# Attention and gated feed-forward on one core: a new place in VectorE's order for three helpers of each unit's last block

## The chip, the cores and the metric

The kernel runs on one core of a Trainium2 chip. The metric is the device time of one execution in microseconds (us), lower is better. The engines are TensorE (PE in the profile, with PEld for its weight loads), VectorE (DVE), ScalarE (ACT), GpSimd (POOL) and SyncE (SP), which issues the transfers.

## The reference, cut to what matters

Attention over 8 batches, 8 heads, 576 positions and 64 values a head, in which a query sees only the 32 keys up to itself (heads 0 to 3) or every fourth of the 128 keys up to itself (heads 4 to 7). Its output, 4608 tokens of 512 values, goes through an RMS norm and a gated feed-forward layer with 1536 hidden values.

```python
scores = where(mask, q @ k.T / 8, -1e9)
x = softmax(scores) @ v                       # to 4608 x 512
xn = x / sqrt(mean(x * x) + 1e-6) * rms_g
g, val = xn @ w_gate, xn @ w_val
out = (g * sigmoid(g) * val) @ w_out
```

## The kernel before, in words

**Units and slots.** The tokens are cut into 16 units u of 288 (half a batch). A unit's feed-forward layer runs over 12 hidden blocks j of 128 values, and each j has three slots of TensorE's order: part 0 is `gate` (12 matmuls into the tile g), part 1 is `val` (12 matmuls into v), part 2 is `proj` of the hidden block before (12 matmuls into four accumulators). At the end of a slot `attend` may add matmuls of the attention of the next unit, so that attention of one unit lies beside the feed-forward layer of the one ahead of it. Each product of the feed-forward layer and, from unit 3 on, of the attention is made of a high and a low part of its operands, which other engines split.

**The order.** It is written out by hand. `later(dt, rank, fn)` (line 435) puts a helper into the list of the slot that is dt slots on; `flush` (line 438) issues that list at the slot's start, sorted by rank, so rank alone decides in which order VectorE and ScalarE get the helpers of one slot. Every engine works through its own list in that order and waits where an operand is not there. What follows a waiting instruction on its engine waits too.

**The hidden block's helpers.** After `gate` of j come, one slot on, the tanh (rank 0, ScalarE, line 816) and `silu` (rank 0.6, VectorE, line 821), both out of g in PSUM; after `val`, one slot on, come `prod` (rank 0, VectorE, line 834: the product of h, th times v) and `parts` (rank 0.5: ScalarE's copy to the high part hhi, line 845, and GpSimd's subtraction to hlo, line 846). The two PSUM banks of g and v alternate: `bank` (line 788) gives g of block j + 1 the bank that v of block j has. So TensorE's first matmul of the next `gate` waits until `prod` has read v.

**The attention's helpers.** A unit has 14 blocks (c, i): for c = 0 and 1 three blocks of 96 queries, for c = 2 and 3 four of 72, each for two heads. A block goes through scores (matmul into the tile s), the softmax's maximum, exponential and normalisation, a transposition of the probabilities, and the output matmul into o. `take` (line 429) sums the parts of o into xraw: from unit 3 on two VectorE instructions for each head (lines 447 and 449), four for a block, at the slot after the output; behind a part-2 slot they have ranks 0.1 and 0.3.

**The turned blocks.** For units 3 to 15 and the blocks (3, 1), (3, 2) and (3, 3) TensorE doesn't transpose; `turn` (line 505) does it with VectorE's transposes of 32 x 64 tiles into a PSUM tile z. In a unit with an even u the band of 72 keys takes 5 such turns a block, with an odd u, where the keys are 104, it takes 6. `turn` is called in the slot of the transposition and leaves three helpers: `squares_of` (VectorE's turns, line 520, one slot on with rank 9, so last in that slot), `hi` (ScalarE's copy of z to the high part of pt, line 525, two slots on, rank 0.2) and `lo` (VectorE's subtraction to the low part of pt, line 529, two slots on, rank 0.9). TensorE's output matmul (line 571) takes both parts. The unit's plan (lines 54 to 60 and 921 to 929) sets these slots, counted from part 0 of j = 0:

| block | turn called | `squares_of` | `hi`, `lo` | output | `take` |
|---|---|---|---|---|---|
| (3, 1) | 17 (part 2) | 18 | 19 | 21 (part 0) | 22 |
| (3, 2) | 19 (part 1) | 20 | 21 | 23 (part 2) | 24 |
| (3, 3) | 21 (part 0) | 22 | 23 | 25 (part 1) | 26 |

Slot 22 is part 1 and slot 23 part 2 of j = 7. The `prod` of j = 7 is in slot 23 with rank 0, `silu` of j = 7 in slot 22 with rank 0.6, and `silu` of j = 8 in slot 25. The turns of block (3, 3) thus stand on VectorE between `silu` and `prod` of j = 7.

The lines that the prediction's steps touch: 429 to 449 (`take`), 505 to 535 (`turn`), 571 (output), 775 and 778 (the matmuls of `gate`, `val`, `proj`), 816 to 846.

Of the kernel before, what the change touches and what calls it, by code (L numbers as in the profile page):

```python
# [62 lines left out]
def geometry(u, c):  # L63


    half = u % 2
    if c < NC // 2:
        if half:
            return [(QB * i, QB * i, 0, P) for i in range(U // QB)], QB, U + W
        return [(QB * i, max(QB * i - W, 0), 0 if i else W, P if i else QB)  # L70
                for i in range(U // QB)], QB, U
    nq = U // DIL
    keys = nq + (W if half else 0)
    return [(nq * r, keys * r, 0 if half else W, keys) for r in range(DIL)], nq, keys * DIL
# [3 lines left out]
def attn_moe(ctx: ExitStack, tc: tile.TileContext, qk_in, v_in, w_gate, w_val, w_out, rms_g, outT):  # L78
# [41 lines left out]
    def later(dt, rank, fn):  # L120
        put_off.setdefault(now[0] + dt, []).append((rank, fn))
# [383 lines left out]
    def turn(b, p):  # L505
        u, c, i = b
        _, nq, _ = geometry(u, c)
        n = geometry(u, c)[0][i][3]
        ng = math.ceil(nq / 32)

        def clear():
            squares_ps[u] = ps.tile([P, 512], F32, tag="s", name=f"z_{u}")[:, :2 * QB].rearrange("k (a q) -> k a q", a=2)
            A.activation(out=squares_ps[u], in_=inv[:, :, None].to_broadcast([P, 2, QB]), func=AF.Copy, scale=0.0)

        def squares_of():
            z = squares_ps[u]
            for g in range(ng):
                for k in (g, g + 1) if u % 2 else (g - 1, g):
                    if k >= 0:
                        V.transpose(out=z[32 * k:32 * (k + 1), :, 32 * g:32 * (g + 1)],  # L520
                                    in_=p[32 * g:32 * (g + 1), :, 32 * k:32 * (k + 1)])

        def hi():
            st[b] = pt = sb.tile([P, 2, 2, QB], F32R, tag="pt", name=f"pt_{u}_{c}_{i}", bufs=2)
            A.copy(out=pt[:n, 0, :, :nq], in_=squares_ps[u][:n, :, :nq])

        def lo():
            pt = st[b]
            V.tensor_tensor(out=pt[:n, 1, :, :nq], in0=squares_ps[u][:n, :, :nq], in1=pt[:n, 0, :, :nq], op=ALU.subtract)

        if i == 1:
            later(1, 7, clear)
        later(1, 9, squares_of)
        later(2, 0.2, hi)
        later(2, 0.9, lo)

    def products(q, t, o, t_ps, s_tag="s", o_tag="o", wait=0):

# [9 lines left out]
        if by_squares:  # L548
            turn(t, p)
# [501 lines left out]
```

## Time and profile before

| | |
|---|---|
| runs | 1111.31, 1114.48, 1116.33 us; median 1114.48 us |
| the profiled execution | 1117.7 us, span 1115.9 us, mean granted clock of TensorE 0.993 |
| busy, share of the span | PE 98%, PEld 96%, DVE 76%, POOL 60%, ACT 56% |
| transfers | 82.18 MB, mean 74 GB/s |

The profiled execution's own time is 1.8 us over its span, and 3.2 us over the median of the runs. Start times in the rows below count from the span's start. In a row of a timeline the columns are start (us), length (us), engine, line, operation, what it writes and reads, shapes and count; a bracket at the end gives the engine's idle time before the instruction and what ended it. Matmuls are pipelined: their lengths overlap, and the distance between their starts is what each costs.

### The profile page before, as it was taken

The numbers are of one execution on the slowest core, as the hardware profiler recorded it, in microseconds if no ns is written. First come the engines' busy times: TensorE is split into PE (matmuls) and PEld (weight loads), VectorE is DVE, ScalarE is ACT, GpSimd is POOL, SyncE is SP. The second block draws the span as 40 slices with busy tenths as digits, with TensorE's granted clock in tenths as the row PEclk, the third lists the DMA queues.
The fourth block names the chain that finished last, engine by engine and source line by source line (L and its number), as shares of the span: only waits on it lengthen the run. The fifth ranks groups of instructions, "written<-read, shape, count | busy, mean of one in ns | idle before, by whom it ended". The sixth has DMA issues, their size and how long they took to land.

```text
span 1115.9 us, 25579 instructions
## 1 busy us (share of the span) xinstructions
PE 1092.2 (98%) x8234; PEld 1067.0 (96%) x8234; DVE 848.9 (76%) x3348; ACT 625.1 (56%) x2241; POOL 672.0 (60%) x1126
## 2 busy tenths in 40 slices
PE   9999999999999999999999999999999999999998
PEld 7787999999999999999999999999999999999998
DVE  6889667878788787887778787787878878788411
ACT  6794676546475564646556464664647556464311
POOL 6333589657585575857657585775758657584311
PEclk9999999999999999999999999999999999999999
DMA  9674213212121121312212131130312112120000
GB/s 257 191 257 171 76 52 91 70 33 81 43 92 52 35 89 42 94 40 58 79 39 84 41 86 52 48 96 26 89 42 87 57 32 86 50 71 13 13 11 22
DMA packets 61544, 82.18 MB, mean 74 GB/s; under 512 B 7298, under 2 KB 41090, under 8 KB 61410
## 3 DMA queue, kind: packets, MB, share of 16 engines
q1 hardware_dynamic: 61410, 80.54, 24.0%
q8 instruction: 66, 1.08, 0.4%
q14 instruction: 68, 0.56, 0.2%
HBM read 71.08 MB, written 9.44 MB: 72 GB/s over the span
## 4 chain that ended last, share of the span: by engine, by line
PE 82%; DVE 13%; issue 2%; ACT 2%; POOL 1%; POOLq 0%; DVEq 0%; ACTq 0%
PE g L778 14%; PE acc L778 14%; PE v L778 14%; PE g L775 8%; PE acc L775 7%; PE v L775 7%; DVE z L520 5%; PE s L583 3%; PE o L571 2%; DVE xraw L447 2%; PE acc L772 2%; PE v L772 2%; PE g L772 2%; DVE xraw L449 2%; PE t L556 1%
## 5 line engine op out<-in xcount | busy, mean ns | idle before, releaser
L846 POOL TENSOR_TENSOR hlo<-th,hhi 128x288 fp32r<-128x288 f32 x179 | 145.1, 811 | 170.6 <-ACT hhi L845 153.3
L425 POOL TENSOR_SCALAR t<-t,sum 96x128 f32<-96x128 f32 (+3 forms) x416 | 150.8, 375 | 112.8 <-DVE sum L419 97.0
L409 ACT ACTIVATE t<-t,sum 96x128 f32<-96x128 f32 (+3 forms) x448 | 166.1, 374 | 92.1 <-DVE sum L394 86.8
L778 PE MATMUL acc<-hhi,lo 128*128 128x288 f32 x720 | 212.5, 295 | 0.0
L778 PE MATMUL g<-xhi,lo 128*128 128x288 f32 x612 | 181.8, 297 | 0.0
L778 PE MATMUL v<-xhi,lo 128*128 128x288 f32 x612 | 181.6, 297 | 0.0
L816 ACT ACTIVATE th<-g 128x288 f32<-128x288 f32 x180 | 74.1, 411 | 173.3 <-PE g L778 132.0
L821 DVE SCALAR_TENSOR_TENSOR th<-th,g 128x288 f32<-128x288 f32 x180 | 80.9, 449 | 96.0 <-ACT th L816 77.4
L447 DVE TENSOR_REDUCE xraw<-o 64x72 f32<-64x144 f32 (+1 forms) x364 | 116.9, 321 | 47.6 <-PE o L571 42.2
L778 PEld LDWEIGHTS acc<-hhi,lo 128*128 128x128 f32 x720 | 135.3, 188 | 0.0
L775 PE MATMUL g<-xhi,hi_g 128*128 128x288 f32 x357 | 108.7, 304 | 16.8 <-DVE th L834 16.8
L845 ACT CAST hhi<-th 128x288 fp32r<-128x288 f32 x180 | 77.7, 432 | 76.9 <-DVE th L834 76.8
L324 POOL TENSOR_TENSOR vhl<-vt,vhl 128x128 fp32r<-128x128 f32 x182 | 84.2, 463 | 59.1 <-ACT vhl L320 30.9
L778 PEld LDWEIGHTS v<-xhi,lo 128*128 128x128 f32 x612 | 116.0, 190 | 0.0
L778 PEld LDWEIGHTS g<-xhi,lo 128*128 128x128 f32 x612 | 115.9, 189 | 0.0
L449 DVE TENSOR_TENSOR xraw<-o,xraw 64x72 f32<-64x72 f32 (+1 forms) x364 | 101.2, 278 | 12.5
L775 PE MATMUL acc<-hhi,hi_o 128*128 128x288 f32 x360 | 107.8, 299 | 0.0
L778 PE MATMUL acc<-hlo,hi_o 128*128 128x288 f32 x360 | 106.5, 296 | 0.0
L834 DVE TENSOR_TENSOR th<-th,v 128x288 f32<-128x288 f32 x180 | 79.8, 443 | 32.3 <-PE v L778 31.7
L363 POOL TENSOR_TENSOR qs<-qk,qs 64x288 fp32r<-64x288 f32 x104 | 84.1, 809 | 19.7 <-ACT qs L358 12.4
L778 PE MATMUL g<-xlo,hi_g 128*128 128x288 f32 x322 | 95.9, 298 | 0.0
L354 POOL TENSOR_TENSOR ks<-qk,ks 128x288 fp32r<-128x288 f32 (+2 forms) x104 | 93.3, 902 | 2.1
(203 smaller groups left out, 3508.9 us busy)
## 6 DMA issues: line engine op xcount, KB each, us to landing
qk<-in_qk_dram SPq DMA_DIRECT2D x60, 288.0 KB, 2.8
vt<-in_v_dram SPq DMA_DIRECT2D x196, 64.0 KB, 1.9
qk<-in_qk_dram SPq DMA_DIRECT2D x30, 352.0 KB, 3.0
out_dram<-ot SPq DMA_DIRECT2D x64, 144.0 KB, 1.9
qk<-in_qk_dram SPq DMA_DIRECT2D x30, 304.0 KB, 2.7
raw<-in_w_gate_dram SPq DMA_DIRECT2D x12, 512.0 KB, 4.6
raw<-in_w_val_dram SPq DMA_DIRECT2D x12, 512.0 KB, 3.3
raw<-in_w_out_dram SPq DMA_DIRECT2D x12, 512.0 KB, 4.1
```

Source lines behind the costliest of these rows:

```text
L324: G.tensor_tensor(out=vp[:, :, 1], in0=vs.pop(b), in1=vp[:, :, 0], op=ALU.subtract)
L354: ek.tensor_tensor(out=ks[:, 1, :nkt], in0=kr, in1=ks[:, 0, :nkt], op=ALU.subtract)
L363: eq.tensor_tensor(out=qs[D:], in0=qr[D:], in1=qs[D:], op=ALU.subtract)
L409: A.activation(out=t[:nq, a, :n], in_=t[:nq, a, :n], func=AF.Exp, scale=-1.0, bias=sm[:nq, a, 0:1], accum_out=None if by_rows(u, c, i) els ...
L425: (V if u == 0 and (c, i) > (NC - 1, 1) else G).tensor_scalar(out=t[:nq, a, :n], in0=t[:nq, a, :n], scalar1=sm[:nq, a, 3:4], scalar2=1.0, ...
L447: V.tensor_reduce(out=ours, in_=o[:D, cols:cols + 2 * nq].rearrange("d (t q) -> d q t", t=2), axis=mybir.AxisListType.X, op=ALU.add)
L449: V.tensor_tensor(out=ours, in0=o[D:, cols:cols + nq], in1=ours, op=ALU.add)
L775: PE.matmul(out, wh[:, cc, :], xh, start=start, stop=False)
L778: PE.matmul(out, w[:, cc, :], v, start=False, stop=stop and k == 1)
L821: V.scalar_tensor_tensor(out=t, in0=t, scalar=1.0, in1=g, op0=ALU.add, op1=ALU.mult)
L834: V.tensor_tensor(out=t, in0=t, in1=v_ps[:, :U], op=ALU.mult)
L846: (V if (u, j) == (NU - 1, NJ - 1) else G).tensor_tensor(out=lo, in0=t, in1=hi, op=ALU.subtract)
```

## The change: what it does

For the last block of each unit, (3, 3), the three helpers of `turn` get other slots and ranks. For block (3, 1) and (3, 2) nothing changes.

```diff
-        later(1, 9, squares_of)
-        later(2, 0.2, hi)
-        later(2, 0.9, lo)
+        last = i == len(geometry(u, c)[0]) - 1
+        later(1 + last, 0.1 if last else 9, squares_of)
+        later(2, 0.55 if last else 0.2, hi)
+        later(2 + last, 0.58 if last else 0.9, lo)
```

In slots: `squares_of` of the last block goes from the end of slot 22 to slot 23 with rank 0.1, just behind `prod`; `hi` stays in slot 23 and goes behind ScalarE's hhi copy; `lo` goes to slot 24 with rank 0.58, behind both halves of `take` of block (3, 2).

## Rows read from the trace of the kernel before

**Rows 1.** The page: busy time by engine, and the chain that ended last

```profile
PE 1092.2 (98%) x8234; PEld 1067.0 (96%) x8234; DVE 848.9 (76%) x3348; ACT 625.1 (56%) x2241; POOL 672.0 (60%) x1126
...
PE 82%; DVE 13%; issue 2%; ACT 2%; POOL 1%; POOLq 0%; DVEq 0%; ACTq 0%
```

**Rows 2.** Waits of PE: line and waited for, us in total, times, longest

```profile
PE g L775 <- DVE th L834: 16.8, 13, 1.7
```

**Rows 3.** Timeline of PE, two units with six turns a block

```profile
361.23 0.35 PE L571 MATMUL o<-pt,vhl 104*128 104x144 f32 x2
361.42 0.34 PE L775 MATMUL v<-xhi,hi_g 128*128 128x288 f32 x1
...
361.86 0.29 PE L775 MATMUL v<-spare,hi_g 128*128 128x288 f32 x1
...
498.96 0.34 PE L571 MATMUL o<-pt,vhl 104*128 104x144 f32 x2
501.02 0.40 PE L775 MATMUL g<-xhi,hi_g 128*128 128x288 f32 x1 [1.71 <-DVE th L834]
...
501.52 0.30 PE L775 MATMUL g<-xhi,hi_g 128*128 128x288 f32 x1
...
504.31 0.35 PE L571 MATMUL o<-pt,vhl 104*128 104x144 f32 x2
```

**Rows 4.** Timeline of PE, a unit with five turns a block

```profile
432.83 0.34 PE L571 MATMUL o<-pt,vhl 72*128 72x144 f32 x2
433.97 0.40 PE L775 MATMUL g<-xhi,hi_g 128*128 128x288 f32 x1 [0.80 <-DVE th L834]
...
434.48 0.30 PE L775 MATMUL g<-xhi,hi_g 128*128 128x288 f32 x1
```

**Rows 5.** Timeline of DVE, the six-turn unit at 500 us

```profile
497.03 0.29 DVE L447 TENSOR_REDUCE xraw<-o 64x72 f32<-64x144 f32 x1
...
498.31 0.45 DVE L821 SCALAR_TENSOR_TENSOR th<-th,g 128x288 f32<-128x288 f32 x1
498.78 1.70 DVE L520 STREAM_TRANSPOSE z<-t 32x64 f32<-32x64 f32 x6
500.51 0.45 DVE L834 TENSOR_TENSOR th<-th,v 128x288 f32<-128x288 f32 x1
500.88 0.30 DVE L529 TENSOR_TENSOR pt<-z,pt 104x144 fp32r<-104x144 f32 x1
```

**Rows 6.** Timeline of DVE, the five-turn unit at 433 us

```profile
432.04 1.40 DVE L520 STREAM_TRANSPOSE z<-t 32x64 f32<-32x64 f32 x5
433.46 0.45 DVE L834 TENSOR_TENSOR th<-th,v 128x288 f32<-128x288 f32 x1
```

**Rows 7.** Timeline of ACT, the six-turn unit at 500 us

```profile
500.51 0.28 ACT L525 CAST pt<-z 104x144 fp32r<-104x144 f32 x1 [3.25 <-DVE z L520]
```

**Rows 8.** Timeline of PE, the six-turn unit at 366 us

```profile
366.70 0.51 PE L775 MATMUL g<-xhi,hi_g 128*128 128x288 f32 x1 [1.71 <-DVE th L834]
...
370.32 0.30 PE L775 MATMUL v<-spare,hi_v 128*128 128x288 f32 x1
```

**Rows 9.** Windows: stretch, length, busy PE, PEld, DVE, ACT, POOL, clock, DMA, GB/s

```profile
200.00:250.00 50.00, 48.29 (x366) 48.13 (x366) 38.67 (x160) 25.09 (x93) 27.91 (x50) 0.97 0.16 45
...
350.00:400.00 50.00, 48.29 (x365) 48.14 (x364) 39.20 (x159) 26.83 (x100) 31.05 (x53) 0.97 0.20 57
400.00:1000.00 600.00, 589.15 (x4616) 587.71 (x4615) 484.61 (x2009) 342.16 (x1267) 397.57 (x680) 1.00 0.21 62
1000.00:1050.00 50.00, 48.28 (x364) 48.14 (x363) 36.25 (x139) 18.86 (x69) 19.97 (x36) 0.97 0.03 9
```

**Rows 10.** Timeline of DVE, the six-turn unit, behind the wait

```profile
503.42 0.46 DVE L821 SCALAR_TENSOR_TENSOR th<-th,g 128x288 f32<-128x288 f32 x1 [1.06 <-ACT th L816]
...
510.51 0.43 DVE L834 TENSOR_TENSOR th<-th,v 128x288 f32<-128x288 f32 x1
```

**Rows 11.** Timeline of PE, the six-turn unit, the gate after the next

```profile
511.57 0.29 PE L775 MATMUL g<-xhi,hi_o 128*128 128x288 f32 x1
```

## The prediction

> **What bounds the kernel now.** I read the page first. TensorE is busy 98% of the span and holds 82% of the chain that ended last [rows 1]; an edit on VectorE can pay only where TensorE stands still. VectorE's 13% of that chain is the lead: there are places where the chain leaves TensorE. The list of TensorE's waits names the place: 13 times the first matmul of a gate waits for the product of h, 16.8 us in all [rows 2]. Units 3 to 15 are 13, seven with six turns a block and six with five. In a six-turn unit the wait is 1.71 us [rows 3, 8], in a five-turn unit 0.80 us [rows 4], and 7 x 1.71 + 6 x 0.80 = 16.8: one wait a unit, always in slot 24, whose gate needs the bank that the product of j = 7 must first read.
>
> VectorE's timeline shows why. Behind silu, at 498.31, come the six turns of the last block, 498.78 to 500.48, and only then the product, 500.51 to 500.96 [rows 5]. TensorE's gate starts 0.06 us after that, at 501.02 [rows 3]. The turns aren't needed until the output of slot 25, so they hold up the earlier deadline for the later one.
>
> **What a wait costs, by starts.** Unhindered, the group behind an output pair starts 361.42 - 361.23 = 0.19 us after it, and its first three matmuls take 0.44 us [rows 3]. In the six-turn unit the gate starts 2.06 us after the pair (498.96 to 501.02), 1.87 late, and its first three take 0.50 (to 501.52) [rows 3]: 1.93 us lost. In the five-turn unit it starts 1.14 after (432.83 to 433.97), 0.95 late, and 0.51 for the first three [rows 4]: 1.02 lost. Sum: 7 x 1.93 + 6 x 1.02 = 13.5 + 6.1 = **19.6 us**.
>
> **What the clock adds.** After the wait at 366 us the next five threes of matmuls take 370.32 - 366.70 = 3.62 us [rows 8], where an unslowed unit takes 0.50 + 4 x 0.40 = 2.10; 0.40 is the step of 12 matmuls from 361.42 on, three at a time, and of the span 501.52 to 504.31, seven threes in 2.79 [rows 3]. So 1.52 us more. The granted clock says what it is: 0.97 in just those three 50 us stretches that hold a six-turn wait followed by slow matmuls, and 1.00 over the 600 us from 400 on [rows 9], in which waits of both kinds lie. [...] 3 x 1.52 = **4.6 us**, which goes if the wait does.
>
> **What the change adds, part by part.**
> The product starts where the turns started: 498.78, ends 0.45 later at 499.23, seen by TensorE 0.06 on, 499.29. The gate's natural start is 498.96 + 0.19 = 499.15. So 0.14 us stay in a six-turn unit. In a five-turn unit the product runs from 432.04 to 432.49 [rows 6] and is seen at 432.55; the natural start is 433.02 [rows 4]: nothing stays, with 0.47 to spare.
>
> The turns follow: 499.26 to 500.96 with six (1.70, rows as now [rows 5]). Then the four sums of block (3, 2), whose output pair ran at 498.96: 1.28 us, the distance from the first sum to silu behind such a four (497.03 to 498.31) [rows 5], so to 502.27. Then the low part, 0.30 [rows 5]: done 502.57, seen 502.63. ScalarE's high part, 0.28 [rows 7], starts when the turns end and lies beside the sums; hhi's copy, now ahead of it, only waits for the earlier product. The output pair of the last block comes 504.31 - 501.02 = 3.29 us after the gate starts [rows 3]: 499.29 + 3.29 = 502.58. So the low part is late by 0.05 us in a six-turn unit. In a five-turn unit all is 0.3 shorter: turns 432.52 to 433.92, sums to 435.22, low part seen at 435.58, output at 433.02 + 3.29 = 436.31: 0.7 to spare.
>
> The order of prod, turns, sums, low part exists nowhere in this trace, so the wait for the low part is a bound from two sides: nothing below, and 1.02 above, a whole five-turn wait of today [rows 4], the nearest wait of TensorE for VectorE. I take 0.05 plus some 0.06 for a disturbed first three, beside 0.14 and another 0.06 at the gate: **0.3 us** a six-turn unit, nearest to nothing because each piece has its length in a row. 7 x 0.3 = 2.1 us stay.
>
> [...] In the rows the instruction behind the product starts 0.37 us after it though the product lasts 0.45 [rows 5], so neighbours on VectorE can overlap by 0.08 us, while turns and product, 498.78 + 1.70 to 500.51, don't. [...]
>
> What is behind the moved pieces: silu of j = 8 now stands behind the low part, from about 502.5, where today VectorE idles 1.06 us ahead of it [rows 10]; its product is then done about 503.4, and the gate of j = 9 comes after three slots, over 5 us from 499.29. The next gate with a margin to watch is that of j = 10: today the product is done at 510.94 [rows 10], the gate starts at 511.57 [rows 11], 0.63 apart. VectorE's chain behind the last sums moves up about as much as TensorE does, some 1.6 us, so this margin stays. ScalarE's high part can hold the tanh of slot 25 by some tenths, but silu, which needs it, is behind the low part anyway. GpSimd gets hhi 1.7 us earlier. No transfer is issued by what moves, and no queue of SP or GpSimd is passed. Same instructions, same count: no busy time is added.
>
> **The sum.** 19.6 + 4.6 - 2.1 = 22.1 us off the profiled execution's 1117.7: 1095.6. Against the median of the runs, 1114.48, the profiled execution is 3.2 us long; part of that may be falls of the clock that the other runs lacked, which nothing here shows. If the median run has three falls the result is 1092.4, if none, 1114.48 - 17.5 = 1097.0. I say 1095.
>
> **The rivals.**
> *The low part becomes the wait.* In the six-turn units TensorE waits at the output of the last block as long as it does today in five-turn units, 1.02 in place of 0.3: 7 x 0.72 = 5 us more, 1100. For it: the low part is last in a chain of eleven VectorE instructions and one of ScalarE, with 0.05 us of lateness as worked. Against: each length is a row.
> *The clock falls all the same.* The waits shrink but the three falls stay: 1095 + 4.6 = 1099.6. Against it: six waits of 0.80 had no fall behind them. [...]
> *Slower.* The low part is late in all 13 units, and the clock falls behind each such wait: 1114.5 - 24.2 + 13 x (1.52 + W). Over 1120 this comes from W = 0.77 us on, that is from a low part some 0.7 us later than worked in six-turn units and 1.4 in five-turn ones. With W of 1.02: 1123. No row shows a fall in a five-turn unit.
> *No effect.* The product is held by something else that ends as late, v's last matmuls or an earlier helper, so that it doesn't move: 1114.5. Against it: VectorE goes from the turns to the product with 0.03 us between and no idle time put down to it [rows 5].
>
> **How the numbers follow.** Forecast 0.72; low part 0.11; clock 0.10; slower 0.03; no effect 0.04. The range starts at 1090, where the median has three falls (1092.4) and nothing stays of the 2.1, and ends at 1103, short of both middle rivals together (1104.6); they lie in it alone. About 0.5%, 5.6 us, is what a measurement of this kernel can tell from no change. The first three cases are faster by more: 0.93; no effect 0.04; slower 0.03.
>
> **What would show it.** Right: TensorE's list of waits has the product of h gone or under 0.3 us each, only in odd units; VectorE's timeline has product, turns, four sums, low part without a gap; granted clock 1.00 from 200 us to 1050; idle time of VectorE ahead of silu of j = 8 gone or smaller. Wrong in a step: a wait of the output (line 571) for the low part of more than 0.5 us; a clock of 0.97 in some stretch; a new wait at the gate of j = 9 or 10. The prediction falls if the time stays above 1103.

## The result and the profile after

The changed kernel takes 1094.41 us, median of 6 runs (1094.31 to 1097.34), where the kernel before took 1114.34 on the same chip; the ratio is 0.9829, 95% interval 0.981 to 0.9848. The profiled execution took 1097.34 us, its span is 1095.6 us. Lines of the kernel from 533 on stand one lower than before: silu is line 822, the product of h 835, the gate's first matmul 776, the output 572.

The page, busy time and the chain that ended last. VectorE's share of the chain went from 13% [rows 1] to 8%: the chain leaves TensorE less often.

```profile
PE 1086.8 (99%) x8234; PEld 1061.9 (97%) x8234; DVE 849.7 (78%) x3348; ACT 624.4 (57%) x2241; POOL 672.4 (61%) x1126
...
PE 86%; DVE 8%; ACT 2%; issue 2%; POOL 2%; DMA 0%; POOLq 0%; DVEq 0%; ACTq 0%; SPq 0%
```

TensorE's waits (line, waited for: us in total, times, longest). The 13 waits for the product of h [rows 2] are gone from the list. The 1.2 us are one wait in unit 0, ahead of 100 us, and the trace of the changed kernel's second run doesn't have it; the edit doesn't touch that unit. It is part of why this execution is 2.9 us over the median.

```profile
PE busy L897 <- ACT ones L95: 2.4, 1, 2.4
PE g L773 <- DVE h L835: 1.2, 1, 1.2
PE t_first L557 <- POOL t L425: 0.3, 1, 0.3
```

VectorE's timeline in a six-turn unit, which answers to [rows 5]. Product, six turns, the sums of the block ahead, low part, silu, in that order.

```profile
361.05 0.46 DVE L822 SCALAR_TENSOR_TENSOR th<-th,g 128x288 f32<-128x288 f32 x1
361.61 0.46 DVE L835 TENSOR_TENSOR th<-th,v 128x288 f32<-128x288 f32 x1
362.10 1.70 DVE L520 STREAM_TRANSPOSE z<-t 32x64 f32<-32x64 f32 x6
363.71 0.28 DVE L447 TENSOR_REDUCE xraw<-o 64x72 f32<-64x144 f32 x1
...
364.98 0.31 DVE L529 TENSOR_TENSOR pt<-z,pt 104x144 fp32r<-104x144 f32 x1
365.20 0.44 DVE L822 SCALAR_TENSOR_TENSOR th<-th,g 128x288 f32<-128x288 f32 x1
```

TensorE's timeline there, which answers to [rows 3]. The gate starts 0.43 us after the output pair (2.06 before, 0.19 unhindered), the last block's output 3.31 us after the gate.

```profile
361.69 0.34 PE L572 MATMUL o<-pt,vhl 104*128 104x144 f32 x2
362.12 0.40 PE L776 MATMUL g<-xhi,hi_g 128*128 128x288 f32 x1
...
362.62 0.30 PE L776 MATMUL g<-spare,hi_g 128*128 128x288 f32 x1
...
365.43 0.42 PE L572 MATMUL o<-pt,vhl 104*128 104x144 f32 x2
365.69 0.36 PE L584 MATMUL s<-ks,qs 128*96 128x192 f32 x2
```

And in a five-turn unit, which answers to [rows 4]: 0.18 us from the output pair to the gate, nothing late.

```profile
426.82 0.34 PE L572 MATMUL o<-pt,vhl 72*128 72x144 f32 x2
427.00 0.34 PE L776 MATMUL g<-xhi,hi_g 128*128 128x288 f32 x1
```

The windows, with columns as in [rows 9]: from 200 us on the granted clock is 1.00 also in the stretches where it was 0.97.

```profile
200.00:250.00 50.00, 49.92 (x390) 49.71 (x389) 41.09 (x169) 26.55 (x100) 30.92 (x55) 1.00 0.16 46
350.00:400.00 50.00, 49.91 (x390) 49.67 (x389) 42.06 (x171) 28.86 (x106) 32.66 (x55) 1.00 0.21 62
400.00:980.00 580.00, 579.71 (x4544) 578.75 (x4544) 477.39 (x1983) 337.16 (x1248) 391.41 (x668) 1.00 0.22 63
980.00:1030.00 50.00, 49.93 (x389) 49.72 (x388) 38.45 (x145) 20.22 (x76) 22.65 (x41) 1.00 0.04 10
```

In the first 50 us it is 0.97 in both traces (before, then after): a fall near 32 us (0.50 from 33 to 35 us before, from 32 to 34 us after), ahead of all that the edit touches.

```profile
0.00:50.00 50.00, 47.25 (x307) 38.50 (x308) 38.90 (x164) 33.13 (x120) 25.71 (x62) 0.97 0.80 219
```

```profile
0.00:50.00 50.00, 47.20 (x308) 38.64 (x309) 39.23 (x165) 33.59 (x120) 25.76 (x62) 0.97 0.81 223
```

### The profile page after: what moved, and what is told of

It is laid out like the page before. It is cut to its first block, busy times and chain, and to the rows that moved or that the text cites. A ratio compares the mean times of both kernels' runs of the same rounds, so it can differ in the third digit from the quotient of the medians.

```text
span 1095.6 us, 25579 instructions
## 1 busy us (share of the span) xinstructions
PE 1086.8 (99%) x8234; PEld 1061.9 (97%) x8234; DVE 849.7 (78%) x3348; ACT 624.4 (57%) x2241; POOL 672.4 (61%) x1126
## 4 chain that ended last, share of the span: by engine, by line
PE 86%; DVE 8%; ACT 2%; issue 2%; POOL 2%; DMA 0%; POOLq 0%; DVEq 0%; ACTq 0%; SPq 0%
PE acc L779 16%; PE g L779 16%; PE v L779 16%; PE g L776 8%; PE acc L776 8%; PE v L776 8%; PE s L584 3%; PE o L572 3%; DVE z L520 2%; PE acc L773 1%; PE t L557 1%; PE g L773 1%; PE v L773 1%; PE s L581 1%; DVE xraw L447 1%
## 5 line engine op out<-in xcount | busy, mean ns | idle before, releaser
L363 POOL TENSOR_TENSOR qs<-qk,qs 64x288 fp32r<-64x288 f32 x104 | 84.2, 810 | 19.6 <-ACT qs L358 12.3
```

The costliest lines, as they stand in the source:

```text
L363: eq.tensor_tensor(out=qs[D:], in0=qr[D:], in1=qs[D:], op=ALU.subtract)
```

## The experiments

**A measure finer than the median.** ScalarE clears z once a unit (line 513). The first clear, ahead of which the edits touch nothing, came between 217.9 and 221.8 us in the profiled executions; it came at 220.7 or later in just the three whose granted clock is 0.97 in the first 50 us. From one clear to the next, though, the spacing repeats to 0.1 us, so it tells small waits apart that medians with that scatter can't. In the changed kernel, run again (median 1094.3 us, ratio 0.9816, 0.9796 to 0.9837), three clears on ScalarE's timeline: 65.11 us over a six-turn unit's last blocks, 65.07 over a five-turn unit's.

```profile
479.26 0.33 ACT L513 ACTIVATE z<-inv 128x192 f32<-128x192 f32 x1
...
544.37 0.33 ACT L513 ACTIVATE z<-inv 128x192 f32<-128x192 f32 x1
...
609.44 0.33 ACT L513 ACTIVATE z<-inv 128x192 f32<-128x192 f32 x1
```

Before the change a five-turn unit's last blocks take 66.13 us and a six-turn unit's 66.66 without a fall of the clock:

```profile
423.20 0.33 ACT L513 ACTIVATE z<-inv 128x192 f32<-128x192 f32 x1
...
489.33 0.33 ACT L513 ACTIVATE z<-inv 128x192 f32<-128x192 f32 x1
...
555.99 0.33 ACT L513 ACTIVATE z<-inv 128x192 f32<-128x192 f32 x1
```

So the change takes 1.55 us off a six-turn unit and some 1.05 off a five-turn one. The two six-turn units with a fall that lie between two clears take 68.2 us, 1.5 more.

> The changed kernel beside the others on one chip: 1094 to 1096 us.

**The turns alone.**

```diff
-        later(2, 0.55 if last else 0.2, hi)
-        later(2 + last, 0.58 if last else 0.9, lo)
+        later(2, 0.2, hi)
+        later(2, 0.9, lo)
```

> The last block's turns stand behind the product as in the changed kernel; its high part keeps rank 0.2 (ahead of hhi's copy on ScalarE) and its low part rank 0.9 in slot 23 (ahead of the sums). Theory A, the place of the turns is all of the gain: 1093 to 1095.5 us, no wait of the gate for the product above 0.3 us, and the output's lateness in six-turn units gone, since the low part comes 1.3 us earlier; hhi's copy waits some 1.7 us for the turns without holding TensorE. Rival B, the order of the high part, sums and low part carries part of the gain: 1099 us or more, with a wait of proj for hlo or of a later gate for a product of h.

Measured: 1099.21 us, ratio 0.986 (0.9836 to 0.9884). Theory A falls: the turns' place brings most of the gain, 16.5 of the 21.4 us by which the repeated changed kernel beats the one before on the same chip, but not all, and B's time came, with waits that B hadn't named. VectorE's timeline has the low part behind an idle 0.34 us, because ScalarE must first make the high part; the four sums come only then and end at 363.22:

```profile
361.74 0.31 DVE L529 TENSOR_TENSOR pt<-z,pt 104x144 fp32r<-104x144 f32 x1 [0.34 <-ACT pt L525]
...
362.93 0.29 DVE L449 TENSOR_TENSOR xraw<-o,xraw 64x72 f32<-64x72 f32 x1
```

TensorE's timeline: the last output comes 3.66 us after its gate, 0.35 more than in the changed kernel.

```profile
359.71 0.40 PE L776 MATMUL g<-xhi,hi_g 128*128 128x288 f32 x1
...
363.37 0.42 PE L572 MATMUL o<-pt,vhl 104*128 104x144 f32 x2 [0.22 <-ACT th L817]
```

The spacing over a six-turn unit is 65.63 us, 0.5 more. The bracket names ScalarE's tanh, which ended last and which the output doesn't read; that was a first hint at two suspects, the sums (o has one buffer) and the chain of hhi, hlo and the values' low part behind the high part.

**The other half alone.**

```diff
-        later(1 + last, 0.1 if last else 9, squares_of)
+        later(1, 9, squares_of)
```

> The other half alone: turns stay in slot 22 ahead of the product, the high part goes behind hhi's copy and the low part to slot 24 behind the sums. Theory A: as before the change, 1112 to 1117 us, with 13 waits of the gate for the product of 1.7 and 0.8 us. Rival B: 1108 us or less.

Measured: 1114.73 us, ratio 0.9998 (0.9981 to 1.0014): as before, with the same waits. The clock falls again behind some of the 1.7 us waits, in the first stretch as in [rows 9], though not in the one from 350 to 400 us: which of them it is differs from trace to trace. From TensorE's waits and the windows:

```profile
PE g L776 <- DVE th L835: 16.7, 13, 1.7
```

```profile
200.00:250.00 50.00, 48.29 (x365) 48.14 (x364) 38.40 (x158) 25.30 (x96) 28.93 (x50) 0.97 0.12 38
```

**Part of the turns ahead.** The list of turns is cut, and three of them stay in slot 22.

```diff
-        later(1 + last, 0.1 if last else 9, squares_of)
+        if last:
+            later(1, 9, lambda: squares_of(slice(3)))
+            later(2, 0.1, lambda: squares_of(slice(3, None)))
+        else:
+            later(1, 9, squares_of)
```

> Three of the last block's turns stay ahead of the product, the rest (three or two) go behind it. Theory A with the price by turns, 0.285 us each: 0.86 us more ahead of the product, so the gate is late by about 1.0 us in six-turn units and 0.4 in five-turn units, in all 7 x 1.07 + 6 x 0.47 = 10.3 us of waits where the changed kernel keeps about 2.8: 1101 to 1103 us, and by A's reading of the clock (it fell only after 1.71 us waits) no fall. Rival C, the clock falls after waits of any length: some stretches at a granted clock of 0.97 and 1.5 us more for each, 1103.5 us or more.

Measured: 1101.77 us, ratio 0.9894 (0.9869 to 0.9919), as theory A has it; 7.5 us over the changed kernel, the very 10.3 - 2.8 of the expectation. The wait goes by the turns that stand ahead of the product, and in the trace the clock didn't fall: 13 waits, none over 0.8 us, and 1.00 in each of the stretches of the windows from 200 us on. Rival C isn't out for all executions, though. One of the ten took 1114.56 us at a mean granted clock of 0.987, with no trace kept. At the 1.52 us a fall of the prediction, its 12.9 us over the others' 1101.7 would be some eight falls (an estimate), so waits this short may let the clock fall too.

```profile
PE g L778 <- DVE th L837: 7.2, 13, 0.8
```

**High part and low part, one at a time.** In the first only `later(2, 0.2, hi)` is as before the change, in the second only `later(2, 0.9, lo)`.

> Turns behind the product and the low part behind the sums as in the changed kernel; only the high part keeps rank 0.2, ahead of hhi's copy. Theory S, what the turns alone lack is that the sums ought to come while ScalarE makes the high part (VectorE stands idle 0.34 us ahead of the low part, the sums end 0.34 us later, and the output of the last block waits for the sums, since o has one buffer): as the changed kernel, 1093.5 to 1095.5 us, six-turn units 65.1 us apart. Theory H, hhi's copy behind the high part holds hlo and the low part of the values on GpSimd, and these hold the output: 1098 to 1100 us, six-turn units 65.6 us.

> Turns behind the product and the high part behind hhi's copy as in the changed kernel; only the low part keeps rank 0.9 in slot 23, ahead of the sums. Theory S: as the turns alone, 1098 to 1100 us, VectorE idle some 0.3 us ahead of the low part and the output of the last block waiting for the sums. Theory H: as the changed kernel, 1093.5 to 1095.5 us.

Measured: 1100.56 us, ratio 0.987 (0.9849 to 0.9891), and 1099.12 us, ratio 0.9861 (0.9838 to 0.9884). S is right on the second and misses the first; H misses the second, and on the first it has the spacing but not the path, since the output isn't late there. Either move alone gains next to nothing over the turns alone. In the second kernel (low part ahead of the sums) the output waits for the sums, named as such on TensorE's timeline, and comes 3.65 us after its gate:

```profile
361.41 0.40 PE L776 MATMUL g<-xhi,hi_g 128*128 128x288 f32 x1
...
365.06 0.42 PE L572 MATMUL o<-pt,vhl 104*128 104x144 f32 x2 [0.19 <-DVE xraw L449]
```

In the first (high part ahead of hhi's copy) the output is 3.31 us after its gate, as in the changed kernel, and the loss lies elsewhere. ScalarE's copy hhi waits behind the high part for the turns, GpSimd's hlo for hhi; th has one buffer, so the tanh of j = 8 waits until hlo has read the product of j = 7, and VectorE stands idle ahead of silu. ScalarE's timeline, then VectorE's:

```profile
362.17 0.41 ACT L817 ACTIVATE th<-g 128x288 f32<-128x288 f32 x1 [0.72 <-POOL hlo L847]
```

```profile
362.61 0.46 DVE L822 SCALAR_TENSOR_TENSOR th<-th,g 128x288 f32<-128x288 f32 x1 [0.52 <-ACT th L817]
```

TensorE pays twice. VectorE is behind from then on, and some 7 us later the gate of j = 10 (369.65), whose margin the prediction watched, loses some 0.2 us to the product of j = 9. Some 11 us later scores of the next unit wait for their queries' low part from GpSimd, which is late too. They take 0.59 us to the next matmul where the repeated changed kernel has 0.23 (this kernel, then that one):

```profile
373.06 0.75 PE L584 MATMUL s<-ks,qs 128*96 128x192 f32 x2
373.65 0.31 PE L776 MATMUL acc<-hhi,hi_o 128*128 128x288 f32 x1
```

```profile
373.04 0.39 PE L584 MATMUL s<-ks,qs 128*96 128x192 f32 x2
373.27 0.32 PE L776 MATMUL acc<-hhi,hi_o 128*128 128x288 f32 x1
```

In the list of the weight loads' waits that is one for each of the six six-turn units that have a next unit, and one more in a five-turn unit:

```profile
PEld s L584 <- POOL qs L363: 2.0, 7, 0.3
```

The spacings over a six-turn unit are 65.65 and 65.52 us; all 12 spacings of a run sum to 4.3 and 2.8 us more than in the repeated changed kernel, which is less than the medians' 6.3 and 4.8. Of that, 1.1 and 0.3 us lie in five-turn units. Some of the rest isn't the edit's: in the second kernel's profile, one of the three with the early fall of the clock, the first clear came 1.9 us later, ahead of all that it touches. The first kernel's profiled execution, 1097.67 us, is the fastest of its five; what made the others longer isn't shown.

**Another buffer for one tanh.** The kernel with the high part ahead of hhi's copy, and:

```diff
-                 sb.tile(..., tag="tmp", ...) if j == NJ - 2 and NEX <= u + 1 < NU else
+                 sb.tile(..., tag="tmp", ...) if j in (8, NJ - 2) and NEX <= u + 1 < NU else
```

> The kernel with the high part ahead of hhi's copy (turns behind the product, low part behind the sums), and the tanh of j = 8 written to another buffer than the one from which GpSimd still reads the product of j = 7. If the cost of the high part's place is that hhi's copy, then hlo, then the one buffer of th hold up the tanh of j = 8 (VectorE idle 0.52 us ahead of silu): that idle time goes, six-turn units come 65.1 to 65.2 us apart, and the time is that of the changed kernel, 1094 to 1096 us. If hlo or the values' low part on GpSimd hold TensorE in another way: 65.6 us and 1097.5 us or more.

Measured: 1094.24 us, ratio 0.9824 (0.9804 to 0.9844), the changed kernel's time. Spacing 65.11 us, and silu of j = 8 follows the low part on VectorE's timeline without idle time:

```profile
361.91 0.31 DVE L529 TENSOR_TENSOR pt<-z,pt 104x144 fp32r<-104x144 f32 x1
362.13 0.45 DVE L822 SCALAR_TENSOR_TENSOR th<-th,g 128x288 f32<-128x288 f32 x1
```

So the one buffer of th is what the high part's old place would have cost.

**A version that beats both.** The same idea one block earlier: the low part of block (3, 2) goes behind the sums of (3, 1) too, ahead of silu in the first kernel (rank 0.57, the diff), behind it in the second (0.61).

```diff
-        later(2 + last, 0.58 if last else 0.9, lo)
+        later(2 + (i > 1), 0.58 if last else 0.57 if i == 2 else 0.9, lo)
```

> The changed kernel, and the low part of block (3, 2) too goes behind the sums of the block ahead of it (slot 22, rank 0.57, ahead of silu). VectorE's idle 0.34 us ahead of that low part goes, silu and the product of j = 7 come 0.3 us or more earlier, and the gate's last 0.24 us in six-turn units and the output's 0.1 with it: 7 x 0.3 to 0.4 us, so 1091.5 to 1092.5 us, six-turn units 64.75 us apart. If what is left in those units is something else (the clock, the matmuls' own length): 1094 us as the changed kernel.

> As the one before, but the low part of block (3, 2) stands behind silu (rank 0.61), between it and the product. In the changed kernel the product starts 0.1 us after silu's end, where other neighbours on VectorE overlap by 0.08. If that is a price of the product reading what silu has just written, an instruction between the two hides it: product 0.1 us earlier than in the one before, by then without effect on the time, 1091.5 to 1092.5 us. If the 0.1 us has another cause it stays, behind the low part.

Measured: 1092.53 us, ratio 0.9807 (0.9784 to 0.983), and 1091.48 us, ratio 0.9801 (0.9777 to 0.9824). The second is the fastest of all. Spacing over a six-turn unit is 64.81 and 64.74 us, so in the second all of the 0.4 us that the changed kernel still loses there is gone. VectorE's timeline of the first and of the second:

```profile
354.31 1.70 DVE L520 STREAM_TRANSPOSE z<-t 32x64 f32<-32x64 f32 x6
356.04 0.30 DVE L447 TENSOR_REDUCE xraw<-o 64x72 f32<-64x144 f32 x1
...
357.34 0.31 DVE L529 TENSOR_TENSOR pt<-z,pt 104x144 fp32r<-104x144 f32 x1
357.56 0.44 DVE L822 SCALAR_TENSOR_TENSOR th<-th,g 128x288 f32<-128x288 f32 x1
358.11 0.46 DVE L835 TENSOR_TENSOR th<-th,v 128x288 f32<-128x288 f32 x1
```

```profile
357.00 0.46 DVE L822 SCALAR_TENSOR_TENSOR th<-th,g 128x288 f32<-128x288 f32 x1
357.37 0.30 DVE L529 TENSOR_TENSOR pt<-z,pt 104x144 fp32r<-104x144 f32 x1
357.59 0.45 DVE L835 TENSOR_TENSOR th<-th,v 128x288 f32<-128x288 f32 x1
```

In the first the product starts 0.11 us after silu's end; in the second the low part stands between, and the product starts 0.59 us after silu's start where it was 0.55 with nothing between: the 0.22 us of the low part cost 0.04. That fits a price of reading what the neighbour has just written, which an instruction between the two hides; what makes it 0.10 us for this pair isn't shown. It did have an effect on the time, against the expectation: the matmul behind the last output still came 0.07 us late in the first kernel and on time in the second.

## Why the prediction was right

**The wait and its cause.** Right: the 13 waits are gone with the turns moved, stay with the rest moved, and go by the number of turns ahead of the product.

**The price of a wait and the clock.** Right, twice over. From the output of slot 23 in unit 3 (230.28 us before, 231.40 after) to the end the span went from 885.6 to 864.2, 21.4 us less; the sum said 22.1. By the clears a six-turn unit got 1.55 us shorter, where 1.93 less 0.40 is 1.53, and a fall cost 1.5. What the trace of before shows of a fall is the granted clock in the windows behind the wait at 366 us: 0.50 from 367 to 370 us and 1.00 from 371 us on, which makes 0.97 over the 50 us (columns as in [rows 9]).

```profile
367.00:368.00 1.00, 1.00 (x6) 1.00 (x6) 0.92 (x4) 0.31 (x2) 0.81 (x2) 0.50 0.00 0
...
369.00:370.00 1.00, 1.00 (x6) 1.00 (x6) 0.00 (x0) 0.06 (x1) 0.00 (x0) 0.50 0.28 78
370.00:371.00 1.00, 1.00 (x9) 1.00 (x8) 0.45 (x1) 0.35 (x1) 0.00 (x0) 0.87 0.04 4
371.00:372.00 1.00, 1.00 (x11) 1.00 (x10) 0.28 (x1) 0.00 (x0) 0.00 (x0) 1.00 0.00 0
```

No stretch of the changed kernel from 200 us on is below 1.00 in its traces, and none of its ten executions has a mean granted clock below 0.998, so for it the rival that the clock falls all the same is out. Why the clock fell after 3 of 7 waits of 1.71 us and not after the others stays open. That it was 0.97 "in just those three" stretches holds from 200 us on only: the first 50 us have it too.

**The forecast of 1095.** In part luck: it is a middle between three falls in the median run of before and none, which the prediction could not choose between. The runs on record tell. The one execution of before that is on record at a granted clock of 1.000 took 1111.22 us, the changed kernel at 1.000 takes 1094.2 to 1094.4, so some 16.9 us go without any fall; 19.6 - 2.8 is 16.8. The median before, 1114.34, lies 3.1 us over that execution, some two falls at 1.52 us.

**What stays in six-turn units.** Mis-sized a little: 0.3 us said, 0.40 measured. The gate is 0.24 late in place of 0.14, because the product starts 0.10 us after silu's end and not right behind it; its first three matmuls take 0.06 more, the output comes 0.02 and the matmul behind it 0.08 late. 7 x 0.40 = 2.8 is just what lies between 19.6 + 4.6 = 24.2 and 21.4. With the overlap of 0.08 us in [rows 5] taken behind the turns too, which the sum left out and the changed kernel's trace shows there (0.09, below), 0.22 would have been said, so the miss is larger than the sum shows. The five-turn units lose nothing, as worked out.

**The joint behind the turns.** In the changed kernel the first sum starts 0.09 us ahead of the turns' end (362.10 + 1.70 against 363.71), where the prediction's sum has no overlap. In the first kernel of the last pair of experiments the first sum of block (3, 1) starts 0.03 us after the end of the turns of block (3, 2) (354.31 + 1.70 against 356.04). What makes the two joints differ isn't shown.

**The low part.** The rival that it becomes the wait is out for the order as changed: TensorE's list has no wait for it, and it costs 0.1 us at most.

**Where the prediction looked past something.** It laid the whole gain on the turns and costed the places of the high part and of the low part at little or nothing. Not wrong for the sum, but the runs show what they are for: the turns alone give 1099.2 where the whole gives 1094.3. The low part behind the sums fills VectorE's 0.34 us of waiting for the high part and lets the one buffer of o come free; the high part behind hhi's copy lets the one buffer of th come free before the next tanh. The buffer of th is shown by the run with another one; that of o is read from a named wait, and no run gave o a second buffer.

## What to carry to other kernels

Where two helpers of one engine stand in one queue, put the one with the earlier deadline first, and read the deadlines from what waits on the tiles, single buffers above all: a late reader of th or o cost 0.4 to 0.5 us a six-turn unit here, where the late product cost 1.9. An instruction that needs another engine's answer to its neighbour (turns, then ScalarE's high part, then the low part) wants independent work in between. To judge such edits, measure from one landmark to the same one a unit later; medians carried falls of the clock at the kernel's start and elsewhere.

## What the runs showed of the hardware that was not expected

In the trace of the changed kernel, from 200 us on, most neighbours on VectorE of which the second doesn't read what the first writes start 0.06 to 0.09 us before the end of the one ahead, as the first sum behind the turns (362.10 + 1.70 to 363.71); others start 0.01 to 0.04 us after it, as the turns behind the product (361.61 + 0.46 to 362.10). Where an instruction reads what its neighbour has just written it started in most pairs 0.03 to 0.04 us after that one's end, as line 654's transposition behind line 477 (237.87 + 0.44 to 238.35). The product behind silu is the odd pair: 0.10 to 0.11 us (361.05 + 0.46 to 361.61; 365.20 + 0.44 to 365.75). The low part between these two cost 0.04 us (0.59 us from silu's start to the product's in place of 0.55).

```profile
237.87 0.44 DVE L477 TENSOR_TENSOR sq<-sq,sq 128x288 f32<-128x288 f32 x1
238.35 0.48 DVE L654 STREAM_TRANSPOSE sqt<-sq 128x288 f32<-128x288 f32 x1
```

From 200 us to the end of the work the granted clock of TensorE fell behind waits of 1.7 us: behind 3 of 7 before the change (0.97 in each one's 50 us), and behind some with the turns left in place (0.97 from 200 to 250 us, 1.00 from 350 to 400). In the trace of the run with three turns ahead it didn't fall behind the 13 waits of 0.8 us or less (mean granted clock 1.000). Whether it can fall behind waits this short stays open: the execution of 1114.56 us at 0.987 has no trace.
